# A Fourier filter and a low-rank mixer on one core: half of the inverse table copied on GpSimd, batch 1's x loaded behind the filters, U prepared earlier

## The chip, the cores and the metric

The kernel runs on one core of a Trainium2 chip. The engines of a core work side by side, each through its own instructions in order: TensorE (PE, matrix products into PSUM), VectorE (DVE), ScalarE (ACT), GpSimd (POOL) and SyncE (SP). POOL and SP also issue the DMAs. The metric is device time in microseconds (us), the median of several executions; lower is better. One further execution was recorded by the hardware profiler.

## The reference

`x` has 8 batches of 3136 x 256 values.

```python
X = np.fft.rfft(x, axis=1)                       # along the 3136
y = np.fft.irfft(X * (filt_r + 1j * filt_i), n=3136, axis=1)
h = y.transpose(0, 2, 1) @ U @ V                 # U: 3136 x 32, V: 32 x 3136
u = y + h.transpose(0, 2, 1)
out = u + np.maximum(u @ w_ch1, 0) @ w_ch2       # 256 -> 1024 -> 256
```

## The kernel before, in words

The transform of length 3136 is done as 64 x 49 by matrix products in float16. **Stage 1** (`pa` for batch 0, `pf` for the others) multiplies x by a 64-point table, `w64`. **Stage 2** (`px`) multiplies by one table per frequency s, `t2`; there are 32 values of s, taken two at a time, so a batch has 16 pairs m = 0 to 15. Then the product with the filters `ft` on VectorE (`uv`), and the inverse of stage 2 (`pi`) with the table `g12`. The inverse of stage 1 is joined with the low-rank part in `make_u`, which gives u (`ut`); `mm1` and `mm2` are the two channel products.

For the product, the real and imaginary halves stand in partitions 0 to 63 and 64 to 127. Batches 0 and 1 multiply by the real and the imaginary filter in one instruction (`both_products`), and apply the inverse with two tables: g and gs, which is g with its halves of partitions swapped. In `g12` g and gs alternate, 98 columns each for every s. Only batches 0 and 1 read gs.

**Loads.** All large loads go through POOL's queue, in the order of the program: x of batch 0 in three chunks (8, 8 and 9 columns of rows); the last rows of the filters; then four parts of eight s each (`PARTS`, lines 231 to 239), every part with its t2, four loads of filters and one load of g12. Batch 1's x comes as `load_x(1, 0)` ahead of the last part, `load_x(1, 1)` and `load_x(1, 2)` behind it, then U (`uq`, with a memset on POOL ahead), V, and the channel weights. `load_table` (178), `load_filters` (185) and `load_x` (146) issue them. Each part of the filters is copied to the other partitions by VectorE (`swap_real` line 213, `swap_imag` line 220) when the pairs reach it.

**Batch 0** (`first_f1`, then `first_mid`, 381). For every pair m the order is: VectorE's product; `back(m - 1)`, the inverse of the pair before (`pi` L395, copied to `et` by ScalarE L398); `ahead(m + 2)`, stage 2 (`px` L488); `first_a(m + 3)`, transposes (`pt` L376, copied by ScalarE L378). From pair 7 on one unit of batch 1's stage 1 is put behind each pair by `next(fill)`. `f1_units` (440) is a generator with 13 units: units 0 to 3 read chunk 0 of x, 4 to 7 chunk 1, 8 to 12 chunk 2. A unit is one product `pf` (L449) and one copy to `asb` (L453 on VectorE, L455 on ScalarE); `asb` has two buffers, one per chunk, and behind the last unit of a chunk SyncE stores it to DRAM (`c1`, L459). The products go to the PSUM tag "o", which has two banks, as do `pt` and `prep_u`'s `pu`.

**The turn** follows the last pair: 25 columns are transposed back (`pe` L432) in seven groups, copied to `e2` by VectorE and ScalarE (L433); behind the second group stands `prep_u` (303), which transforms U (L311, L321), and behind groups 1 to 4 the last four units. Then `h1_unit` (`ph` L566) forms the low-rank part of batch 0 and `make_u(0)` the first u (`pu` L618 and L624, two copies to `ut` L676).

**Then the main loop**, from `mm1` L683 on: two pairs of instructions of `mm1` and `mm2` alternate with units of later batches at slots (`sched`). Batch 1's pairs start at slot 8, in the second group of rows. Their input `a` (L469, SyncE) is read from `c1`, and each of its loads reads rows of all three chunks; SyncE issues its DMAs in order.

Of the kernel before, what the change touches and what calls it, by code (L numbers as in the profile page):

```python
# [26 lines left out]
def _consts():  # L27
    n, half = SEQ, SEQ // 2
    r = np.array([8 * (k // 4) + 4 * h + k % 4 for h in range(2) for k in range(NH - h)])
    q = np.arange(NQ)  # L30


    w = np.zeros((NQ, NS, 2))
    for s in range(NS):
        w[:, s, 0] = np.cos(2 * np.pi * s * q / NQ)
        w[:, s, 1] = -np.sin(2 * np.pi * s * q / NQ)
    w[:, 0, 1] = (-1.0) ** q
    w = w.reshape(NQ, 64)
    turn = np.arange(64).reshape(4, 16).T.ravel()
    w64 = np.zeros((128, 128))  # L40
    w64[:64, :64] = w
    w64[64:, 64:] = w
    s2 = np.zeros((128, 128))
    s2[:64, :64] = w.T / ESC
    s2[64:, 64:] = w.T / ESC


    t2 = np.zeros((NS, 98, 128))
    g = np.zeros((NS, 128, 98))
    for s in range(NS):  # L50
        for j in range(49):
            if j < 25:
                f = s + 64 * j
                e, sg = np.exp(-2j * np.pi * f * r / n), 1.0
            elif s:
                f = 64 * (j - 24) - s
                e, sg = np.exp(-2j * np.pi * (n - f) * r / n), -1.0
            else:
                f = 32 + 64 * (j - 25)
                e, sg = np.exp(-2j * np.pi * f * r / n), 1.0  # L60
            ei = np.conj(e)
            if s:
                t2[s, :49, j], t2[s, 49:, j] = e.real, -e.imag
                t2[s, :49, 64 + j], t2[s, 49:, 64 + j] = sg * e.imag, sg * e.real
                g[s, j] = np.concatenate([ei.real, ei.imag]) * 2
                g[s, 64 + j] = np.concatenate([-ei.imag, ei.real]) * 2 * sg
            else:
                o = 0 if j < 25 else 49
                t2[s, o:o + 49, j] = e.real
                t2[s, o:o + 49, 64 + j] = e.imag  # L70
                g[s, j, o:o + 49] = ei.real * (2 if f else 1)
                g[s, 64 + j, o:o + 49] = -ei.imag * 2

    t2[0, :, 64] = 0
    t2[0, 49:, 64] = (-1.0) ** r
    g[0, 64] = 0
    g[0, 64, 49:] = (-1.0) ** r
    g *= ESC / n
    gs = np.concatenate([g[:, 64:], g[:, :64]], 1)
    f16 = np.float16  # L80
    return (w64.astype(f16), s2.astype(f16), np.eye(128).astype(f16),
            np.tile(np.eye(32), (4, 4)).astype(f16),
            np.pad(np.hstack([w[:, turn], w[:, turn].T / ESC]), ((0, 64), (0, 0))).astype(f16),
            np.ascontiguousarray(t2.reshape(4, 8, 98, 128).transpose(0, 2, 1, 3)).astype(f16),
            np.ascontiguousarray(np.stack([g, gs], 1).reshape(4, 8, 2, 128, 98)
                                 .transpose(0, 3, 1, 2, 4)).astype(f16))


@with_exitstack
def kernel(  # L90
# [10 lines left out]
):  # L101
    nc = tc.nc
    nb = x.shape[0]
    w64_np, s2_np, idn_np, fold_np, wp_np, t2_np, g_np = _consts()
    w64_d = nc.inline_tensor(w64_np, name="w64d")
    s2_d = nc.inline_tensor(s2_np, name="s2d")
    idn_d = nc.inline_tensor(idn_np, name="idnd")
# [1 line left out]
    wp_d = nc.inline_tensor(wp_np, name="wpd")  # L109
    t2_d = nc.inline_tensor(t2_np, name="t2d")  # L110
    g_d = nc.inline_tensor(g_np, name="gd")
    RD = NR * DM
    c1 = [nc.dram_tensor(f"c1_{b}", (64, RD), F16, kind="Internal") for b in range(nb)]
    c2 = [nc.dram_tensor(f"c2_{b}", (64, RD), F16, kind="Internal") for b in range(nb)]
# [62 lines left out]

    def load_table(k, a, b):

        dst, src, w = ((t2, t2_d, 128), (g12, g_d, 196))[k]  # L180
        n, p = (b - a) * w, dst.shape[0]
        nc.gpsimd.dma_start(dst[:, a * w:b * w],
                            bass.AP(tensor=src, offset=a // 8 * p * n, ap=[[n, p], [1, n]]))

    def load_filters(a, b):

# [42 lines left out]
    s2 = cst.tile([128, 128], F16)  # L229
    nc.sync.dma_start(s2, s2_d.ap())  # L230
    for k, part in enumerate(PARTS):
        if k == 3:
            load_x(1, 0)
        if k:
            load_table(0, *part)
        load_filters(*part)
        if k == 0:
            load_table(0, *part)
        load_table(1, *part)
    load_x(1, 1)  # L240
    load_x(1, 2)
    uq = sb.tile([128, NR * RANK], F16, tag="esb", bufs=2, name="uq")
    nc.gpsimd.memset(uq[64:128, :], 0.0)
    nc.gpsimd.dma_start(uq[0:64, :], moe_U.rearrange("(q r) p -> q (r p)", q=NQ))
    vqs = []
    for k in range(2):
        v = sb.tile([128, SEQ // 2], F16, tag="xt", bufs=5, name="vq")
# [55 lines left out]
    def prep_u():  # L303
        usb = sb.tile([128, NH * RANK], F16, tag="uv", bufs=3, name="usb")
        st[0]["usb"] = usb
        nc.vector.memset(usb[64:128, (NH - 1) * RANK:NH * RANK], 0.0)
        for n0, nn in ((0, 16), (16, 9)):
            pu = bank("o", "pu")
            for h in range(2):
                k = nn // 4  # L310
                nc.tensor.matmul(  # L311
                    pu[64 * h:64 * h + 64, 0:4 * k * RANK], w64[0:64, 0:64],
                    bass.AP(tensor=uq.tensor, offset=uq.offset + (2 * n0 + 4 * h) * RANK,
                            ap=[uq[0:64, :].ap[0], [8 * RANK, k], [1, 4 * RANK]]),
                    start=True, stop=True, skip_group_check=True)
            if nn % 4:
                nc.tensor.matmul(pu[0:64, (nn - 1) * RANK:nn * RANK], w64[0:64, 0:64],
                                 uq[0:64, (NR - 1) * RANK:NR * RANK],
                                 start=True, stop=True, skip_group_check=True)
            m = (min(nn, NH - 1 - n0)) * RANK  # L320
            nc.scalar.copy(usb[:, n0 * RANK:n0 * RANK + m], pu[:, 0:m])  # L321
            if m < nn * RANK:
                nc.vector.tensor_copy(usb[0:64, n0 * RANK + m:(n0 + nn) * RANK],
                                      pu[0:64, m:nn * RANK])
# [56 lines left out]
    def first_mid(fill):  # L381
# [5 lines left out]
        def back(m, uv):  # L387
            pi = bank("fx"[m % 2], "pi")
            for sl in range(2):
                for dh in range(2):  # L390
                    for fi in range(2):
                        g = (4 * m + 2 * sl + fi) * 98
                        o = fi * 512 + sl * DM + dh * 128
                        a = (dh * 2 + sl) * 98
                        nc.tensor.matmul(pi[:, a:a + 98], uv[:, o:o + 128], g12[:, g:g + 98],  # L395
                                         start=(fi == 0), stop=(fi == 1), skip_group_check=True)
            for h in range(2):
                nc.scalar.copy(  # L398
                    etv[:, h, :, 0:NH - h, 4 * m:4 * m + 4],
                    pi[:, 0:392].rearrange("p (e k r) -> p e r k", e=2, r=NR)  # L400
                    [:, :, h * NH:h * NH + NH - h])
# [6 lines left out]
        for m in range(NS // 2):  # L408
            for k, part in enumerate(PARTS):
                if k and 2 * m == part[0]:  # L410
                    swap_real(*part)
                    swap_imag(*part)
            uv = both_products(m, pxs.pop(0))
            if pend is not None:
                back(*pend)
            pend = (m, uv)
            if m + 2 < NS // 2:
                pxs.append(ahead(m + 2))
            if m + 3 < NS // 2:
                first_a(m + 3)  # L420
            if m >= 7:
                next(fill)
        back(*pend)
        e2 = new_e2(0, 0)
        for k4, n0 in enumerate(range(0, NH, 4)):
# [3 lines left out]
            for rr in range(w):  # L429
# [2 lines left out]
                    nc.tensor.transpose(pt[0:k, o:o + 128], et[:, a:a + k], idn[:, :])  # L432
            (nc.scalar.copy if k4 in (1, 4, 6) else nc.vector.tensor_copy)(  # L433
                split(e2[0:k, n0 * DM:(n0 + w) * DM]), natural(pt[0:k, 0:w * DM]))
            if k4 == 1:
                prep_u()
            if k4 in (1, 2, 3, 4):
                next(fill)

    def f1_units(b, both):  # L440
        ne = 0
        for c in range(len(CH)):
            xt = st[b]["x"].pop(c)
            asb = sb.tile([128, 9 * DM], F16, tag="asb", bufs=2, name="asb")
            for n0 in range(0, CH[c], 2):
# [3 lines left out]
                nc.tensor.matmul(pf[:, 0:w], w64[:, :], xt[:, n0 * DM:n0 * DM + w],  # L449
                                 start=True, stop=True)  # L450
                dst = asb[0:k, n0 * DM:n0 * DM + w]
                if both and ne % 2 and (b > 1 or ne >= 9):
                    nc.vector.tensor_copy(dst, pf[0:k, 0:w])  # L453
                else:
                    nc.scalar.copy(dst, pf[0:k, 0:w])  # L455
# [59 lines left out]
    def stream():  # L515
        pend = []

        def i1(b, m, y, esb):
            pi = bank("f", "pi")
            nf = 2 if b == 1 else 1  # L520
            for sl in range(2):
                for fi in range(nf):
                    g, o = (4 * m + 2 * sl + fi) * 98, fi * 512 + sl * DM
                    nc.tensor.matmul(pi[0:98, sl * DM:(sl + 1) * DM], g12[:, g:g + 98],  # L524
                                     y[:, o:o + DM], start=(fi == 0), stop=(fi == nf - 1),
                                     skip_group_check=True)
# [121 lines left out]
    def make_u(gx):  # L648
# [11 lines left out]
        for dh in range(2):  # L660
# [12 lines left out]
                nc.scalar.copy(dst.rearrange("p (k h r t) -> p k h r t", k=2, h=2, r=4),  # L673
                               pm.rearrange("p (r h k t) -> p k h r t", r=4, h=2, k=2))
            else:
                nc.scalar.copy(dst, pm)  # L676

    def mm1(gx, t):
        w = groups[gx][2] * 128
# [105 lines left out]
    h1gen = h1_unit(0)  # L785
    next(h1gen)
    make_u(0)

    steps = [7.6 + 1.3 * k for k in range(NP)] + [28 + 2.45 * k for k in range(NP)]
    for b in range(3, nb):  # L790
# [86 lines left out]
```

## Time and profile before

| what | value |
|---|---|
| runs | 539.4, 538.82, 539.82 us; median 539.4 |
| the profiled execution | 541.74 us, its span 540.0 us |
| mean granted TensorE clock | 0.982 |
| TensorE busy | 501.7 us, 93% of the span, 4022 products |
| VectorE, ScalarE, GpSimd busy | 400.1, 377.3, 288.5 us |
| DMA | 94.58 MB, mean 175 GB/s |
| chain that ended last | TensorE 76%, VectorE 9%, DMA 6%, ScalarE 4% |

The span runs from the first to the last instruction of the profiled execution; 541.74 us is its whole time. Times in the views count from the start of the span. In the slices of the page each digit is a fortieth of the span (13.5 us), in tenths; PEclk is the clock that TensorE was granted, 9 being 0.9 or more. In a timeline the number in brackets is how long the engine stood idle ahead of the instruction, and what ended that.

### The profile page before, as it was taken

How to read it: one execution, taken by the hardware profiler on the slowest of the kernel's cores; microseconds unless marked ns; L12 is line 12 of the kernel's file. 1: busy time of each engine (PE TensorE's matmuls, PEld its weight loads, DVE VectorE, ACT ScalarE, POOL GpSimd, SP SyncE). 2: the span in 40 equal slices, each digit the busy share in tenths (PEclk: the TensorE clock that was granted, in tenths of full speed). 3: DMA queues.
4: the chain of work that ended last, by engine and by line, in shares of the span. 5: the costliest groups of instructions: out<-in, count | busy, mean ns of one | idle time of the engine just before them, and what ended most of it. 6: DMA issues, size and time to landing. Idle time of an engine off the chain costs nothing.

```text
span 540.0 us, 11365 instructions
## 1 busy us (share of the span) xinstructions
PE 501.7 (93%) x4022; PEld 305.3 (57%) x4022; DVE 400.1 (74%) x576; ACT 377.3 (70%) x768; POOL 288.5 (53%) x406
## 2 busy tenths in 40 slices
PE   3856899999999999999999999999999999999995
PEld 3745557767666776555555555555555555454444
DVE  6876367676887767887888878887899887336664
ACT  2746676667676768878878878887777777775541
POOL 7657634344466455666677657774656565313000
PEclk9968799999999999999999999999999999999999
DMA  8999898966988649997989788996786684554324
GB/s 132 179 179 191 163 207 226 199 205 171 239 195 226 183 97 252 213 221 179 202 205 233 192 170 214 208 226 150 187 197 159 133 189 116 133 109 80 73 67 104
DMA packets 118426, 94.58 MB, mean 175 GB/s; under 512 B 52961, under 2 KB 100770, under 8 KB 118370
## 3 DMA queue, kind: packets, MB, share of 16 engines
q0 software_dynamic: 21936, 42.52, 39.6%
q1 hardware_dynamic: 96434, 51.35, 37.8%
q8 instruction: 31, 0.51, 0.4%
q14 instruction: 25, 0.20, 0.1%
HBM read 56.85 MB, written 48.17 MB: 194 GB/s over the span
## 4 chain that ended last, share of the span: by engine, by line
PE 76%; DVE 9%; DMA 6%; ACT 4%; issue 3%; POOL 1%; DVEq 0%; ACTq 0%; SPq 0%; POOLq 0%
PE phh L683 26%; PE po L739 20%; PE po L709 8%; PE px L488 5%; PE pi L524 4%; DVE uv L509 4%; PE pu L609 3%; PE pf L449 3%; DMA xt<-in_x_dram 3%; PE ph L566 2%; ACT h L691 2%; DVE uv L507 2%; DMA g<-gd 2%; DMA c<-asb 1%; PE po L713 1%
## 5 line engine op out<-in xcount | busy, mean ns | idle before, releaser
L691 ACT ACTIVATE h<-phh 128x512 f16<-128x512 f32 (+1 forms) x382 | 201.6, 578 | 73.7 <-PE phh L683 69.2
L683 PE MATMUL phh<-ut,w 128*128 128x512 f16 x768 | 197.6, 379 | 1.0 <-ACT ut L676 0.5
L512 POOL TENSOR_TENSOR y<-uv 128x512 f16<-128x512 f16 x96 | 113.2, 1180 | 108.8 <-DVE uv L509 71.4
L739 PE MATMUL po<-h,w 128*128 128x512 f16 x560 | 143.8, 379 | 0.0
L509 DVE TENSOR_TENSOR uv<-px,ft 64x512 f16<-64x512 f32 x192 | 132.1, 688 | 2.6
L683 PEld LDWEIGHTS <-w 128*128 128x128 f16 x832 | 78.4, 98 | 77.8 <-issue 3.1
L752 POOL DMA_DIRECT2D out_dram<-och x120 | 69.7, 588 | 46.5 <-DVE och L744 43.3
L528 ACT CAST esb<-pi 98x512 f16<-98x512 f32 x112 | 65.9, 588 | 37.8 <-PE pi L524 34.3
L507 DVE TENSOR_TENSOR uv<-px,ft 128x512 f16<-128x512 f32 x96 | 64.8, 675 | 36.2 <-PE px L488 34.0
L739 PEld LDWEIGHTS <-w 128*128 128x128 f16 x560 | 51.6, 98 | 53.2 <-issue 1.1
L743 DVE TENSOR_TENSOR tt<-po,ut 128x512 f32<-128x512 f32 x70 | 48.4, 692 | 41.3 <-PE po L739 30.1
L709 PE MATMUL po<-w,h 128*128 128x256 f16 x448 | 58.1, 273 | 0.0
L488 PE MATMUL px<-a,t 98*128 98x256 f16 x256 | 50.3, 278 | 6.7 <-DVE uv L509 4.7
L455 ACT CAST asb<-pf 128x512 f16<-128x512 f32 (+1 forms) x83 | 48.0, 579 | 10.6 <-PE pf L449 7.6
L744 DVE STREAM_TRANSPOSE och<-tt 128x512 f32<-128x512 f32 x70 | 49.8, 711 | 2.4
L709 PEld LDWEIGHTS <-h 128*128 128x128 f16 x448 | 42.5, 98 | 10.3 <-issue 1.1
L496 DVE TENSOR_TENSOR uv<-px,ft 128x1024 f16<-128x1024 f32 x32 | 38.2, 1220 | 12.3 <-PE px L488 11.9
L488 PEld LDWEIGHTS <-t 98*128 98x128 f16 x256 | 22.1, 100 | 34.8 <-DVE uv L509 17.0
L449 PE MATMUL pf<-xt,w 128*128 128x512 f16 (+1 forms) x91 | 35.0, 386 | 5.4 <-DMA xt<-in_x_dram 4.6
L673 ACT CAST ut<-pu 128x512 f16<-128x512 f32 x70 | 38.1, 608 | 0.7 <-PE pu L609 0.7
L524 PE MATMUL pi<-y,g 128*98 128x256 f16 x192 | 36.7, 272 | 0.5 <-POOL y L512 0.5
L153 POOL DMA_DIRECT2D xt<-in_x_dram x50 | 30.3, 612 | 5.1 <-DMA xt<-in_x_dram 2.4
(92 smaller groups left out, 448.1 us busy)
## 6 DMA issues: line engine op xcount, KB each, us to landing
xt<-in_x_dram POOLq DMA_DIRECT2D x46, 256.0 KB, 6.8
a<-c SPq DMA_DIRECT2D x28, 384.0 KB
c<-esb SPq DMA_DIRECT2D x28, 384.0 KB
e<-c SPq DMA_DIRECT2D x56, 192.0 KB
out_dram<-och SPq DMA_DIRECT2D x160, 64.0 KB
c<-asb POOLq DMA_DIRECT2D x30, 256.0 KB, 4.2
out_dram<-och POOLq DMA_DIRECT2D x120, 64.0 KB, 3.3
out_dram<-och POOLq DMA_DIRECT2D x24, 256.0 KB, 5.3
```

The source lines that it names most:

```text
L449: nc.tensor.matmul(pf[:, 0:w], w64[:, :], xt[:, n0 * DM:n0 * DM + w], start=True, stop=True)
L488: nc.tensor.matmul(px[:, sl * DM:(sl + 1) * DM], t2[:, s * 128:(s + 1) * 128], a2[:, (2 * ml + sl) * DM:(2 * ml + sl + 1) * DM], start=Tru ...
L507: nc.vector.tensor_mul(uv[:, 0:512], px[:, :], ft[:, a:a + 512])
L509: nc.vector.tensor_mul(uv[p:p + 64, 512:1024], px[q:q + 64, :], ft[q:q + 64, b:b + 512])
L512: nc.gpsimd.tensor_add(y, uv[:, 0:512], uv[:, 512:1024])
L524: nc.tensor.matmul(pi[0:98, sl * DM:(sl + 1) * DM], g12[:, g:g + 98], y[:, o:o + DM], start=(fi == 0), stop=(fi == nf - 1), skip_group_che ...
L528: nc.scalar.copy(split(esb[:, ml * 512:(ml + 1) * 512]), natural(pi[0:98, :]))
L683: nc.tensor.matmul(pm[:, 0:w], w1[:, dh * 1024 + t * 128:dh * 1024 + (t + 1) * 128], ut[:, dh * w:(dh + 1) * w], start=(dh == 0), stop=(dh ...
L691: nc.scalar.activation(h[:, 0:w], pm[:, 0:w], RELU)
L709: nc.tensor.matmul(po[:, o:o + DM], hs[gx, t][:, rr * 128:(rr + 1) * 128], w2[:, t * DM:(t + 1) * DM], start=(t == 0), stop=False, skip_gr ...
L739: nc.tensor.matmul(po[:, :], w2[:, t * DM + dh * 128:t * DM + (dh + 1) * 128], hs[gx, t][:, :], start=(t == 0), stop=(t == 7))
L752: (nc.gpsimd if k and b < nb - 1 else nc.sync).dma_start(dst, och[32 * i:32 * i + 32, k * 512:(k + 1) * 512] .rearrange("p (r e) -> p r e" ...
```

## The change

- `g12` holds all of g first and all of gs behind it. Only part 0 of gs is loaded; for parts 1 to 3 POOL copies the two halves of g to the swapped partitions (`swap_table`: two copies of 64 partitions x 784 elements a part), each part's copies being one part later in POOL's order than its load.
- `load_x(1, 0)` moves behind the last part; U's load comes right behind it, and its memset goes to VectorE. The last swap stands ahead of `load_x(1, 2)`.
- Units of batch 1's stage 1 start at pair 9. Unit 7 and `prep_u` come ahead of the last `back`, units 8 and 9 behind groups 2 and 4 of the turn, and units 10 to 12 behind `make_u(0)`.
- VectorE copies units 8 to 11 (before 9 and 11), the second part of `usb` and the second half of the first `ut`, which ScalarE copied before.

```diff
     def load_table(k, a, b):
-        dst, src, w = ((t2, t2_d, 128), (g12, g_d, 196))[k]
+        dst, src, w = ((t2, t2_d, 128), (g12, g_d, 98))[k]
 ...
+    def swap_table(a, b):
+        o = NS * 98
+        for p, q in ((0, 64), (64, 0)):
+            nc.gpsimd.tensor_copy(g12[p:p + 64, o + a * 98:o + b * 98],
+                                  g12[q:q + 64, a * 98:b * 98])
 ...
     for k, part in enumerate(PARTS):
-        if k == 3:
-            load_x(1, 0)
         if k:
             load_table(0, *part)
         load_filters(*part)
         if k == 0:
             load_table(0, *part)
         load_table(1, *part)
+        if k == 0:
+            nc.gpsimd.dma_start(g12[:, NS * 98:(NS + 8) * 98], gs_d.ap())
+        if k > 1:
+            swap_table(*PARTS[k - 1])
+    load_x(1, 0)
+    uq = sb.tile([128, NR * RANK], F16, tag="esb", bufs=2, name="uq")
+    nc.vector.memset(uq[64:128, :], 0.0)
+    nc.gpsimd.dma_start(uq[0:64, :], moe_U.rearrange("(q r) p -> q (r p)", q=NQ))
     load_x(1, 1)
+    swap_table(*PARTS[3])
     load_x(1, 2)
-    uq = sb.tile([128, NR * RANK], F16, tag="esb", bufs=2, name="uq")
-    nc.gpsimd.memset(uq[64:128, :], 0.0)
-    nc.gpsimd.dma_start(uq[0:64, :], moe_U.rearrange("(q r) p -> q (r p)", q=NQ))
 ...                                                    # prep_u
-            nc.scalar.copy(usb[:, n0 * RANK:n0 * RANK + m], pu[:, 0:m])
+            (nc.vector.tensor_copy if n0 else nc.scalar.copy)(usb[:, n0 * RANK:n0 * RANK + m], pu[:, 0:m])
 ...                                                    # first_mid: back; the same in i1
-                        g = (4 * m + 2 * sl + fi) * 98
+                        g = (fi * NS + 2 * m + sl) * 98
 ...                                                    # first_mid: the pairs and the turn
-            if m >= 7:
+            if m >= 9:
                 next(fill)
+        next(fill)
+        prep_u()
         back(*pend)
 ...
-            if k4 == 1:
-                prep_u()
-            if k4 in (1, 2, 3, 4):
+            if k4 in (2, 4):
                 next(fill)
 ...                                                    # f1_units
-                if both and ne % 2 and (b > 1 or ne >= 9):
+                if both and (ne % 2 if b > 1 else 8 <= ne < 12):
 ...                                                    # make_u
-                nc.scalar.copy(dst, pm)
+                (nc.vector.tensor_copy if gx == 0 and dh else nc.scalar.copy)(dst, pm)
 ...                                                    # after the first u
     make_u(0)
+    for k in range(3):
+        next(fill)
```

More of the change, by code (lines that the diff above doesn't have):

```diff
@@ L84, in _consts @@
             np.ascontiguousarray(t2.reshape(4, 8, 98, 128).transpose(0, 2, 1, 3)).astype(f16),
-            np.ascontiguousarray(np.stack([g, gs], 1).reshape(4, 8, 2, 128, 98)
-                                 .transpose(0, 3, 1, 2, 4)).astype(f16))
+            np.ascontiguousarray(g.reshape(4, 8, 128, 98).transpose(0, 2, 1, 3)).astype(f16),
+            np.ascontiguousarray(gs[0:8].transpose(1, 0, 2)).astype(f16))
 @with_exitstack
@@ L103 @@
     nb = x.shape[0]
-    w64_np, s2_np, idn_np, fold_np, wp_np, t2_np, g_np = _consts()
+    w64_np, s2_np, idn_np, fold_np, wp_np, t2_np, g_np, gs_np = _consts()
     w64_d = nc.inline_tensor(w64_np, name="w64d")
@@ L111 @@
     g_d = nc.inline_tensor(g_np, name="gd")
+    gs_d = nc.inline_tensor(gs_np, name="gsd")
     RD = NR * DM
@@ L522, in i1 @@
                 for fi in range(nf):
-                    g, o = (4 * m + 2 * sl + fi) * 98, fi * 512 + sl * DM
+                    g, o = (fi * NS + 2 * m + sl) * 98, fi * 512 + sl * DM
                     nc.tensor.matmul(pi[0:98, sl * DM:(sl + 1) * DM], g12[:, g:g + 98],
```

## The prediction

> **What bounds the kernel now.** I read the page's slices first. Before slice 6 (13.5 us each) TensorE has gaps and loses its clock; behind it TensorE is almost full, and the windows view gives it 445.45 us busy of the 460 us from 80 to 540. So the change, which touches the first 75 us alone, is worth what it shifts the start of that full stretch.
>
> ```profile
> PE   3856899999999999999999999999999999999995
> PEclk9968799999999999999999999999999999999999
> ```
>
> Then TensorE's timeline of that stretch (start, length, engine, operation, in brackets the idle time ahead and what ended it):
>
> ```profile
> 36.93 0.61 PE L449 MATMUL pf<-xt,w 128*128 128x512 f16 x1 [4.11 <-DMA xt<-in_x_dram]
> ...
> 40.77 0.63 PE L449 MATMUL pf<-xt,w 128*128 128x512 f16 x1
> ...
> 52.46 1.76 PE L432 MATMUL pe<-idn,et 128*128 128x128 f16 x16 [3.58 <-ACT et L398]
> ...
> 55.81 0.59 PE L449 MATMUL pf<-xt,w 128*128 128x512 f16 x1 [0.78 <-ACT usb L321]
> ...
> 60.42 1.19 PE L566 MATMUL ph<-e,usb 128*32 128x256 f16 x25
> ...
> 72.20 0.38 PE L488 MATMUL px<-a,t 98*128 98x256 f16 x2
> ```
>
> Three gaps: the first unit of batch 1 stands in pair 7 and waits 4.11 us for batch 1's x; the turn waits 3.58 us; `prep_u` holds it for another 0.78. ScalarE's timeline names the cause of the second, unit 8, which waits for the store of chunk 0 to free its `asb` buffer, with the last `et` copy queued behind it:
>
> ```profile
> 51.37 0.59 ACT L455 CAST asb<-pf 128x512 f16<-128x512 f32 x1 [2.13 <-DMA c<-asb]
> ```
>
> Then the DMA issues, one window for each issue, which give issue and landing; the second half of `load_x(1, 0)` is issued at 28.33 and lands 8.6 later, at 36.93:
>
> ```profile
> xt<-in_x_dram POOLq DMA_DIRECT2D x1, 256.0 KB, 8.6
> ```
>
> From such rows POOL's loads land one behind the other, in the order of issue: the first 8 filters by 18.2, t part 0 18.9, g 0 21.5, t 1 22.7, filters 1 25.5, g 1 28.0, t 2 28.9, filters 2 32.7, g 2 34.2, x(1,0) 36.9, t 3 38.0, filters 3 40.6, g 3 42.4, x(1,1) 44.5, x(1,2) 47.1. POOL issues a load as soon as the one eight places ahead has landed (27th 21.85 after the 19th at 21.5, 33rd 28.33 after the 25th at 28.0), so the transfers are the bound and not the issuing.
>
> **The change part by part: table and x.** A part of g shrinks from 392 to 196 KB. t has 196 KB, and its steps above are 0.7, 1.2, 0.9 and 1.1 us; I take 1.1. The g steps are 2.6, 2.5, 1.5 and 1.8, so each part saves 0.4 to 1.5, together with g 2 some 2.2. Part 0 gains nothing (g and gs, two loads for one). x(1,0) now comes behind t 3 (1.1), filters 3 (2.6) and a halved g 3 (1.1): 36.9 + 4.8 - 2.3 = 39.4. It is needed in pair 9 instead of 7. Against pair 9's unit in the old run (40.77) that is 1.4 us sooner. TensorE still stands idle there, from about 35.5 (pair 8's product is ready at 34.5, one DVE step of 1.2 behind the filters' swap that ends at 33.3; its inverse and the transforms behind it take 1) to 39.4.
>
> **The copies.** No POOL copy here changes partitions, so the price is bounded by three rows:
>
> ```profile
> L272 POOL COPY low<-vq 32x256 f16<-32x256 f16 x12 | 8.2, 725 | 2.8 <-DMA vq<-in_moe_V_dram 2.8
> ...
> L549 POOL COPY low<-wp 64x448 f16<-64x448 f16 x7 | 3.9, 570 | 0.1
> ...
> L781 POOL COPY w<-w2n 128x1024 f16<-128x1024 f16 x2 | 2.0, 1033 | 2.5 <-DMA w2n<-in_moe_w_ch_dram 2.5
> ```
>
> The last two give 0.8 ns an element and 0.21 us fixed: 0.84 for 784 elements. At L272's 2.8 ns it would be 2.2; at no less than 570 for 448 it can't go under 0.57. I take 0.84, the contiguous rows being the nearest: 1.7 a swap. Swap 1 waits on POOL for g 1, now 26.7, and ends at 28.5; queued behind it are t 3 and all of filters 3. Pair 4's product ends at 28.3 already, so its inverse starts about 0.2 late, which DVE, two pairs ahead, hides. Swap 2 waits for g 2 (about 32) and ends at 34; pair 8 needs it at 34.4. Behind it are the x loads: issued at 34.1 and 34.7, they find three or four microseconds of filters still in the queue, so 39.4 stands. Swap 3 ends near 39, and pair 12 needs it after 41; queued behind it are x(1,2), V and the weights. V is issued at 42.95 now; the swaps fill POOL's waits for landings, the transfers ahead are 2.3 shorter and the memset is gone, so it will be issued no later, while its readers come at most 4 sooner; V's copies end at 59.3 now and only their first rows are needed for the first u. The memset of `uq` goes from POOL (1.43) to DVE, where it falls into the idle 3.11 us ahead of 14.07; uncovered it would cost 0.7 (a DVE memset of 32x1024 words is 0.91).
>
> The copies also meet DVE's own copies. One row shows such a meeting: the swap of filters at 41.84 took 1.03 instead of 0.69 beside POOL's memset (40.88 to 42.31). DVE has over a microsecond to spare at the swaps of parts 2 and 3, as TensorE waits for x. POOL can be held as well: 0.3 at swap 1 (DVE's copies end at 27.0, g 1 lands at 26.7) and 0.8 at swap 2 (DVE's end at 33.3, POOL's begin at 32.5), 1.1 for four copies, which the queue still covers. The Trainium skill (SBUF — State Buffer, section Who interferes with whom) says that such a DVE copy and a GpSimd instruction lock each other out of a shared port for a whole instruction, which speaks against this change. By that rule the row would have been 1.16, so the trace nearly agrees.
>
> **From pair 9 to the turn.** Pairs 10 and 11 go at the slow clock's step, as the old ones did (36.93, 38.83, 40.77): 1.9 each. Pair 12 is bound by ScalarE's three copies, 1.6; 13 lacks `first_a`, 1.1; 14 and 15 take 0.95 (asb and the et copies, 47.21 to 48.11). That is 8.4 to unit 6, at 47.8. Then ScalarE has et, two asb, a usb and the last et to do, with `prep_u` on TensorE between, as its two banks come free: 3.3. The first transposes start at 51.1, 1.4 before the old 52.46. The wait for chunk 0's store is gone, since unit 8 now stands in the turn.
>
> **The turn** took 60.5 - 52.46 = 8.0. `prep_u` leaves it (54.28 to 55.81, 1.5) and two of four units (0.43 and 0.11). At half clock throughout it would be 50 transposes (0.85 for 8) and two units: 6.2. At full clock DVE's six copies of 0.69 and their dispatch bind: 4.9. I take 5.2. Gain 2.8; `ph` starts 4.2 sooner.
>
> **Beside the first u.** Three units now stand between `make_u(0)` and the first `phh`. They have two banks: unit 12 waits until DVE has copied u's second half (0.69) and unit 10 (0.69). On the old clock times: u's second half ready 63.5, DVE done with unit 10 at 64.95, unit 12 on TensorE to 65.1, then `phh`, then unit 12's copy on ScalarE, and the first h at 65.8 instead of 64.76. Loss 1.0; the copy of u halved between two engines (0.5) is in it.
>
> **Who waits next.** Batch 1's `a` loads need the whole of c1, so they come behind the store of the last chunk. SyncE's timeline:
>
> ```profile
> 61.04 1.08 SPq L459 DMA_DIRECT2D c<-asb  x2
> 65.35 5.17 SPq L469 DMA_DIRECT2D a<-c  x6
> ```
>
> The store went out when unit 12 was copied (61.02), 3.7 before the first h; the loads 4.3 later; their queue shows the first tile's 512-byte packets until about 69.5, so it is there by 69.9, 2.3 ahead of the `px` at 72.20. Now unit 12 is copied at the first h. The slack of 2.3 turns into a wait of 1.4 (0 to 2.5).
>
> **Sum.** 1.4 + 2.8 - 1.0 - 1.4 = 1.8 sooner. The profiled execution took 541.74 (span 540.0); the runs' median is 539.4, 2.3 less. 541.74 - 1.8 = 539.9, less 2.3: 537.6. A change of 0.2% (1.1 us) is about what can be told from none.
>
> **Rivals.** *The clock stays full.* TensorE's granted clock fell to 0.55 in 52 to 59, after the gap of 3.58, and the gaps left in the turn are under 1 us; but it also fell (0.59 from 28 to 32) after a gap of 1.3. If only long gaps count, the turn is 4.9, and with pair 9's wait a little shorter pairs 10 and 11 go at 1.6: 0.3 + 0.6 more, 536.7. The Trainium skill (TensorE: Matmul & The Clock Gate, Part 1) has this rule: half clock after a whole idle window of about 3.4 us. By that rule the old turn agrees, and the drop at 28 doesn't. Chance 0.2.
>
> *The late units eat it all.* If the last store shares the queue with x(2,1), which is issued at about the same time, `a` lands another 1 to 2 us later; that leaves -0.2 to 0.8, in the middle 539.1. For it: both queues' packets lie close together from 61 to 69 now. Chance 0.14.
>
> *The copies hold up POOL.* At 2.2 us a copy (L272's rate) swap 1 ends at 31.2, swap 2 at 39.3, the filter queue runs dry, and x(1,0), issued at 39.3 and 39.9, lands 4.0 later (as lightly queued x loads do at 63): 43.9, 4.5 later than in the forecast, with TensorE idle all the while: 537.6 + 4.5 = 542.1, slower. It decides from 0.84 + 1.8 / 4 = 1.3 us a copy, four copies being ahead of x. For it: the change of partitions, and DVE's copies, which alone bring a copy to 0.84 + 1.1 / 4 = 1.12; against it: the rows of 570 and 1033. Chance 0.24, half copies included.
>
> **How the numbers follow.** Forecast 0.42, with its own range 536.9 to 538.4 (transfer steps and the turn's bounds); clock 0.2, eaten 0.14, copies 0.24. Faster 0.62, same 0.14, slower 0.24. The range reaches from 535.0 (clock, and no wait for `a`) to 541.0 (copies of about 1.7 us).
>
> **What would show it.** Right: POOL copies near 0.84; unit 0 in pair 9 waiting 3 to 4 us for x until about 39.4; no ScalarE wait for c in the turn; transposes from about 51; `phh` about 3 sooner; `px` waiting 1 to 2 for `a`. Wrong: copies over 1.3, x after 41, or no wait at `px`.

## The result, and the profile after

The new kernel's median is 541.21 us (11 runs) against 538.81 for the old one in the same rounds: ratio 1.0052, 95% interval 1.0029 to 1.0074. It is slower by some 2.4 us; 537.6 was forecast. Two later rounds gave 1.0050 (1.0027 to 1.0072) and 1.0038 (1.0008 to 1.0068). The old kernel measured against itself gave 1.0036 (1.0008 to 1.0063) and 1.0004 (0.9972 to 1.0036), so a single ratio may stray by more than its interval says; three of the same sign stand. The ratios use undisturbed executions alone, so they are not the quotients of the medians beside them.

The profiled execution of the new kernel took 540.77 us, 0.4 under its median, its span 538.8. The page's slices again:

```profile
PE   4758879999999999999999999999999999999995
PEclk9989899999999999999999999999999999999999
```

Laid beside the slices of before, they do not show a slower kernel: the clock is lost for less time. TensorE's timeline (start, length, operation, idle time ahead and what ended it):

```profile
39.02 0.59 PE L461 MATMUL pf<-xt,w 128*128 128x512 f16 x1 [4.45 <-DMA xt<-in_x_dram]
...
50.00 1.51 PE L446 MATMUL pe<-idn,et 128*128 128x128 f16 x24 [0.64 <-ACT et L410]
...
55.59 0.38 PE L578 MATMUL ph<-e,usb 128*32 128x256 f16 x5 [0.79 <-DVE e L447]
...
59.14 0.27 PE L461 MATMUL pf<-xt,w 128*128 128x256 f16 x1 [0.84 <-DVE asb L465]
...
71.29 0.39 PE L500 MATMUL px<-a,t 98*128 98x256 f16 x2 [2.54 <-DMA a<-c]
```

Unit 0 waits for x until 39.02, the transposes begin at 50.0 (forecast: 39.4 and 51.1), unit 12 waits for its bank, `px` waits 2.54 for `a`: much of the forecast's picture. Against the recorded old execution `px` is 0.9 us sooner (71.29 against 72.20). The runs say the opposite, so the recorded old execution is what has to be looked at.

GpSimd's copies, from the groups of its operations (count, busy us, mean ns, idle ahead), and SyncE's timeline:

```profile
L190 POOL COPY g<-g 64x784 f16<-64x784 f16 x6 | 5.7, 947 | 0.3
```

```profile
59.88 1.08 SPq L471 DMA_DIRECT2D c<-asb  x2
67.42 2.46 SPq L481 DMA_DIRECT2D a<-c  x6
```

Unit 8's wait for chunk 0's store has moved from ScalarE to VectorE and is smaller (in the two other recordings of the new kernel, below, it is 0.27 and nothing):

```profile
53.05 0.69 DVE L465 CAST asb<-pf 128x512 f16<-128x512 f32 x1 [0.80 <-DMA c<-asb]
```

### The profile page after: what moved, and what is told of

Same layout as the page of the kernel before. It is cut to its first block, busy times and chain, and to the rows that moved or that the text cites. A ratio compares the mean times of both kernels' runs of the same rounds, so it can differ in the third digit from the quotient of the medians.

```text
span 538.8 us, 11373 instructions
## 1 busy us (share of the span) xinstructions
PE 499.2 (93%) x4022; PEld 302.0 (56%) x4022; DVE 403.1 (75%) x581; ACT 375.4 (70%) x764; POOL 293.7 (55%) x412
## 4 chain that ended last, share of the span: by engine, by line
PE 74%; DVE 10%; DMA 6%; ACT 4%; issue 3%; POOL 3%; SPq 0%; DVEq 0%; ACTq 0%; POOLq 0%
PE phh L695 26%; PE po L751 19%; PE po L721 8%; PE px L500 5%; PE pi L536 4%; DVE uv L521 4%; PE pu L621 3%; PE pf L461 3%; DMA xt<-in_x_dram 2%; DVE uv L519 2%; PE ph L578 2%; ACT h L703 2%; DMA c<-asb 1%; DMA ft<-in_filt_r_dram 1%; PE po L725 1%
## 5 line engine op out<-in xcount | busy, mean ns | idle before, releaser
L703 ACT ACTIVATE h<-phh 128x512 f16<-128x512 f32 (+1 forms) x382 | 201.8, 578 | 74.7 <-PE phh L695 69.9
L467 ACT CAST asb<-pf 128x512 f16<-128x512 f32 (+1 forms) x81 | 46.9, 582 | 10.8 <-PE pf L461 10.7
L721 PEld LDWEIGHTS <-h 128*128 128x128 f16 x448 | 42.5, 98 | 10.3 <-issue 1.1
L461 PE MATMUL pf<-xt,w 128*128 128x512 f16 (+1 forms) x91 | 33.8, 375 | 5.8 <-DMA xt<-in_x_dram 4.4
L621 PEld LDWEIGHTS <-e 96*128 96x128 f16 x686 | 26.5, 98 | 10.7 <-DVE e L589 1.7
```

Of the source, the lines that this page charges most:

```text
L703: nc.scalar.activation(h[:, 0:w], pm[:, 0:w], RELU)
L721: nc.tensor.matmul(po[:, o:o + DM], hs[gx, t][:, rr * 128:(rr + 1) * 128], w2[:, t * DM:(t + 1) * DM], start=(t == 0), stop=False, skip_gr ...
```

## The experiments

Each run here took 12 executions (the first comparison 11), one of them recorded. Kernels of a round ran in turn on one chip, with the old one between them. In the table "x" is when unit 0 of batch 1 starts on TensorE, "store" when the last store of c1 is issued, "px" batch 1's first `px`, all from the one recorded execution, whose time is in the second column; "rest" is its span less px. That execution can lie some us above or below the median: those of the first old one, `a_table`, `s_slot` and `m_early` took 2.2 to 2.9 us more than the median, those of `u_late` and `n_loaded` 1.9 to 2.4 less, and that of `ctl_before` 3.6 less, so their times of x, store and px are not typical ones.

| kernel | recorded | x | store | px (its wait for a) | rest | median, ratio (interval) |
|---|---|---|---|---|---|---|
| old, first recorded | 541.74 | 36.93 | 61.04 | 72.20 (0) | 467.8 | 538.81 |
| old, `c_before` | 538.13 | 33.49 | 54.09 | 67.66 (2.25) | 468.7 | 539.37, 1.0036 (1.0008 to 1.0063) |
| old, `ctl_before` | 536.18 | 33.15 | 54.56 | 66.56 (0.68) | 467.8 | 539.82, 1.0004 (0.9972 to 1.0036) |
| new, first recorded | 540.77 | 39.02 | 59.88 | 71.29 (2.54) | 467.5 | 541.21, 1.0052 (1.0029 to 1.0074) |
| new, `c_after` | 541.23 | 38.85 | 60.56 | 70.88 (2.73) | 468.2 | 541.10, 1.0050 (1.0027 to 1.0072) |
| new, `ctl_after` | 541.50 | 39.10 | 60.10 | 70.73 (3.03) | 468.8 | 541.31, 1.0038 (1.0008 to 1.0068) |
| `a_table` | 541.02 | 33.83 | 57.53 | 71.28 (2.44) | 468.0 | 538.31, 0.9990 (0.9958 to 1.0022) |
| `b_turn` | 537.32 | 38.72 | 56.91 | 68.11 (0.66) | 467.5 | 537.40, 0.9975 (0.9958 to 0.9993) |
| `u_late` | 538.93 | 32.64 | 58.01 | 68.49 (2.84) | 468.6 | 541.31, 1.0015 (0.9991 to 1.0039) |
| `n_loaded` | 539.72 | 37.72 | 58.94 | 69.17 (1.38) | 468.4 | 541.63, 1.0026 (1.0006 to 1.0045) |
| `s_slot` | 541.55 | 38.99 | 60.17 | 73.80 (0) | 465.6 | 539.32, 0.9994 (0.9971 to 1.0017) |
| `m_early` | 542.76 | 34.58 | 53.49 | 70.88 (0) | 469.9 | 540.06, 1.0001 (0.9976 to 1.0025) |
| `l_turn` | 537.96 | 39.01 | 56.60 | 67.66 (0.52) | 468.4 | 538.84, 0.9997 (0.9968 to 1.0026) |
| `p_early` | 537.16 | 32.24 | 54.69 | 66.62 (1.40) | 468.5 | 537.50, 0.9980 (0.9950 to 1.0009) |

`c_before`, `c_after`, `a_table` and `b_turn` shared a round (the old kernel's median beside them 538.08), as did `u_late` to `m_early` (540.12), and `ctl_before`, `ctl_after`, `l_turn` and `p_early` (539.48). Medians compare within these three groups.

**The old kernel again.** No edit.

> The old kernel again, unchanged. Theory one (the recorded execution of the old kernel was a late one: 541.74 us against a median of 538.81, while the new one's, 540.77, was no later than its median of 541.21): most executions of the old kernel reach batch 1's first px two to three microseconds sooner than 72.2, so at 69 to 70.5, because x(1,0) lands sooner or the clock is lost for less time; span about 537. Theory two (the start is as recorded, and the loss of the new kernel lies behind px, in the main loop): px again at 72.2 +- 0.5, and the stretch from px to the end is shorter than the 467.8 recorded for the old kernel. Ratio 1.000 either way.

TensorE's timeline of this execution:

```profile
33.49 0.39 PE L449 MATMUL pf<-xt,w 128*128 128x512 f16 x1 [1.42 <-DMA xt<-in_x_dram]
...
47.95 1.07 PE L432 MATMUL pe<-idn,et 128*128 128x128 f16 x16 [1.37 <-ACT et L398]
...
67.66 0.38 PE L488 MATMUL px<-a,t 98*128 98x256 f16 x2 [2.25 <-DMA a<-c]
```

Theory one holds: x is there 3.4 us sooner than in the first recording, the gap ahead of the turn is 1.37 instead of 3.58, and `px` comes at 67.66, sooner than the 69 to 70.5 expected, and already waits for `a`. This execution took 1.2 us less than the median of its run, so it is itself a somewhat early one. The ratio of 1.0036 was not expected.

**The new kernel again.** No edit.

> The new kernel again, unchanged. Both theories: ratio 1.003 to 1.007. Theory one: px at 71 to 72, having waited 2 to 3 us for a, and 467.5 +- 0.7 us from px to the end, as recorded (538.8 - 71.3). Theory two: from px to the end 469 or more.

px at 70.88 (0.1 under the expected band), 468.2 behind it (at the band's upper end), against 468.7 and 467.8 in the old kernel. Nothing is lost in the main loop that these recordings show; the difference stands in when px starts, on average 71.0 in three recordings of the new kernel and 67.1 in the two further ones of the old. Already the first `phh` starts at 59.25 to 59.92 in the new kernel's three, against 56.91 and 57.38 in the old one's two.

**The table alone** in the old kernel (`swap_table` and the columns of `g12` as in the change).

```diff
-        dst, src, w = ((t2, t2_d, 128), (g12, g_d, 196))[k]
+        dst, src, w = ((t2, t2_d, 128), (g12, g_d, 98))[k]
...
+        if k == 0:
+            nc.gpsimd.dma_start(g12[:, NS * 98:(NS + 8) * 98], gs_d.ap())
+        if k > 1:
+            swap_table(*PARTS[k - 1])
     load_x(1, 1)
+    swap_table(*PARTS[3])
```

> The table alone: halved g, gs copied by GpSimd; x(1,0) stays ahead of the last part, the units in pairs 7 to 15, prep_u and the last units in the turn. If the saved transfers count, x(1,0) lands about 2.2 sooner than in the old kernel, the wait in pair 7 shrinks by that, and the ratio is 0.996 to 0.998. If GpSimd's copies hold up what is queued behind them (measured 0.85 to 1.0 a copy, so 1.7 to 2.1 a swap), x is no sooner: 1.000. If the copies are what makes the new kernel slower: above 1.003.

x lands at 33.6, no sooner than in the old kernel (33.1 and 33.3 in the two further recordings), though its second half is issued only at 28.84 (25.6 and 26.1 there), behind the first swap. Unit 0 starts at 33.83 without a wait, and the ratio is 0.9990: the second of the three outcomes by the time of x. The ratio alone does not exclude the first, as its interval reaches from 0.9958 to 1.0022.

**The three late units back in the turn.**

```diff
-            if k4 in (2, 4):
+            if k4 in (2, 3, 4, 5, 6):
                 next(fill)
...
     make_u(0)
-    for k in range(3):
-        next(fill)
```

> The new kernel with units 10 to 12 back in the turn (units 8 to 12 behind groups 2 to 6), none behind make_u(0). Theory of the late a (the new kernel loses at px, where it waited 2.5 us, and 1 us at the first h): the turn grows by 1 to 1.5 (three units more on VectorE and ScalarE), the wait at px shrinks from 2.5 to under 0.7, the first h comes 1 us sooner behind make_u(0); the time falls by 1.5 to 2.5 against the new kernel, ratio 0.998 to 1.003. If the loss lies elsewhere (the main loop, the copies), the ratio stays at 1.004 to 1.006.

The last store leaves 3.6 us sooner than in `c_after`, `px` waits 0.66 instead of 2.73 and comes 2.8 sooner; the median falls by 3.7 in the same round, and the ratio of 0.9975 is just below the expected band. SyncE's and TensorE's lines:

```profile
56.91 1.09 SPq L471 DMA_DIRECT2D c<-asb  x2
68.11 0.38 PE L500 MATMUL px<-a,t 98*128 98x256 f16 x2 [0.66 <-DMA a<-c]
```

The late units are the part of the change that costs.

**The late units alone** in the old kernel.

```diff
-            if k4 in (1, 2, 3, 4):
+            if k4 == 1:
                 next(fill)
...
     make_u(0)
+    for k in range(3):
+        next(fill)
```

> The old kernel with one thing alone: units 10 to 12 behind make_u(0) instead of in the turn. Theory of the late a (batch 1's first px starts when the chain last unit, store, loads of a is through; the later last unit moves px, and everything behind px only shifts): the last store goes out 4 to 6 us later than in the old kernel seen from the first phh, px waits 4 to 6 us for a (old kernel: 0 and 2.3 in two recorded executions), ratio 1.004 to 1.010. Rival (the new kernel's copies and x order cost, the late units don't): the turn is 1 us shorter and the ratio is 0.998 to 1.002.

The wait is 2.84, less than expected, and the ratio 1.0015 leaves no clear verdict. The last store leaves 3.5 to 3.9 later than in the old kernel's two further recordings, but `px` follows it by 10.5 instead of 12.0 to 13.6. So a cost of the late units by themselves is not shown, nor excluded (the interval ends at 1.0039); within the new kernel, where x is late as well, they cost what `b_turn` shows. The late x alone was not run.

**All of gs loaded, nothing copied.** (`gs_d` then holds all of gs.)

```diff
-        if k == 0:
-            nc.gpsimd.dma_start(g12[:, NS * 98:(NS + 8) * 98], gs_d.ap())
-        if k > 1:
-            swap_table(*PARTS[k - 1])
+        a, n = part[0], 8 * 98
+        nc.gpsimd.dma_start(g12[:, (NS + a) * 98:(NS + a + 8) * 98],
+                            bass.AP(tensor=gs_d, offset=k * 128 * n, ap=[[n, 128], [1, n]]))
...
-    swap_table(*PARTS[3])
```

> The new kernel with all of gs loaded and none copied: everything else of the change as it is. If the saved transfers count as forecast, x(1,0) lands 2 to 2.5 us later than the new kernel's 38.9, at 41 to 41.5, and the ratio is 1.008 to 1.011. If GpSimd's copies let the queue of transfers run thin (the DMA share over 30 to 40 us is 0.90 in the new kernel and 1.15 in the old one), x lands within 1 us of 38.9 and the ratio is that of the new kernel, 1.004 to 1.007.

Unit 0 has x at 37.72, 1.3 sooner than in the first new recording with 588 KB more ahead of it, so the saved transfers saved nothing. The windows view of 20 to 40 us (busy time and instructions of each engine; the last three columns are granted clock, DMA share and GB/s), the old kernel (`ctl_before`), the new one (`ctl_after`) and this one in turn:

```profile
20.00:40.00 20.00, 13.43 (x173) 11.04 (x171) 19.45 (x19) 13.74 (x38) 14.41 (x24) 0.97 1.14 193
```

```profile
20.00:40.00 20.00, 12.86 (x160) 10.81 (x158) 19.57 (x20) 11.57 (x32) 18.41 (x28) 0.91 0.89 152
```

```profile
20.00:40.00 20.00, 14.55 (x168) 12.21 (x168) 19.39 (x21) 12.87 (x34) 16.38 (x28) 0.87 1.08 201
```

With copies the DMA engines carry 152 GB/s, without them 193 and 201; the seven recordings with copies lie between 151 and 161, the others between 192 and 209, the first old recording at 169. Part of the difference is the saving itself: 588 KB over 20 us are 29 GB/s. For the rest GpSimd's timeline of the new kernel shows a place: no load is issued while the copies run.

```profile
25.32 0.62 POOL L183 DMA_DIRECT2D g<-gd  x1
25.99 1.71 POOL L190 COPY g<-g 64x784 f16<-64x784 f16 x2
27.64 0.59 POOL L183 DMA_DIRECT2D t<-t2d  x1
...
30.57 0.82 POOL L183 DMA_DIRECT2D g<-gd  x1
31.43 2.02 POOL L190 COPY g<-g 64x784 f16<-64x784 f16 x2
33.39 1.21 POOL L154 DMA_DIRECT2D xt<-in_x_dram  x2
```

x, issued at 33.4 and 34.0, finds an almost empty queue (the last load ahead of it lands at 34.5), and its second half lands 4.9 later (7.2 to 8.6 in the three old recordings, behind a full one). Without the copies x is issued 2.9 and 2.4 us sooner and takes longer, 6.0 for the second half:

```profile
30.53 0.67 POOL L154 DMA_DIRECT2D xt<-in_x_dram  x1
31.57 0.83 POOL L154 DMA_DIRECT2D xt<-in_x_dram  x1 [0.37 <-DMA t<-t2d]
```

In time, 1.0026 is under the expected band and under the new kernel's ratios, but those come from other rounds; what the copies cost in the end is open.

**Batch 1's pairs two slots later.**

```diff
-    steps = [7.6 + 1.3 * k for k in range(NP)] + [28 + 2.45 * k for k in range(NP)]
+    steps = [10 + 1.14 * k for k in range(NP)] + [28 + 2.45 * k for k in range(NP)]
```

> The new kernel with batch 1's pairs put from slot 10 (step 1.14) instead of 7.6 (1.3): the first px stands two slots later in TensorE's order, behind products of the channel layers. If what is lost is TensorE standing idle in front of px, the wait of 2.5 us shrinks to under 1 and the time falls by 1 to 2 us against the new kernel: ratio 1.001 to 1.004. If the loss is in when the stream of batch 1 starts and not in TensorE's idling (its pairs then meet later slots), the ratio stays at 1.004 to 1.007.

px stands at 73.80 and waits for nothing; the rest is 465.6, so TensorE did other work meanwhile. The ratio, 0.9994, is under the expected band, which speaks for TensorE's idle time ahead of px as what the new kernel loses. The new kernel did not run in this round, and the same shift was not tried in the old kernel, where px can wait for `a` too.

**x early, with the rest of the change.** `b_turn` with

```diff
+        if k == 3:
+            load_x(1, 0)
...
-    load_x(1, 0)
+    load_x(1, 1)
     uq = sb...
-    load_x(1, 1)
     swap_table(*PARTS[3])
...
-            if m >= 9:
+            if 7 <= m < 15:
                 next(fill)
-        next(fill)
         prep_u()
```

> A combination: the new table, U and the split copies; x(1,0) ahead of the last part and x(1,1) ahead of U, units 0 to 7 in pairs 7 to 14, units 8 to 12 in the turn, none behind make_u(0). Theory of the late a: the last unit and so the last store go out 2 to 3 us sooner than in the kernel with the units back in the turn (56.9), a and px as much sooner (px at 65 to 66.5 against 68.1): ratio 0.992 to 0.996. If the chain is not bound by the units but by the queue of transfers (the store and a behind the channel weights), px stays at 67.5 to 68.5: 0.997 to 0.999.

The last store goes out at 53.49, sooner than in any other kernel, and `px` is no sooner for it (70.88). In this execution other transfers take the place: the first `phh` waits for the channel weights, a unit of batch 2 for its x.

```profile
57.80 1.05 PE L695 MATMUL phh<-ut,w 128*128 128x512 f16 x4 [2.57 <-DMA w<-in_moe_w_ch_dram]
64.73 0.38 PE L461 MATMUL pf<-xt,w 128*128 128x512 f16 x1 [2.04 <-DMA xt<-in_x_dram]
```

It was the longest of its twelve, 2.7 us over the median, so whether these waits stand in the others is not shown. The ratio of 1.0001 shows no gain either way.

**Controls, and the change without its two suspects.** `l_turn` joins the edits of `n_loaded` and `b_turn`; `p_early` is `l_turn` with the x order of `m_early`.

> The old kernel unchanged, beside the three others on one chip, as the measure of how far the ratio strays by itself (it was 1.0036 once): 0.997 to 1.003. The recorded execution: x(1,0) at 33 to 37, px at 67.5 to 72.5, 467.5 to 468.7 behind it.

> The new kernel unchanged on the same chip: 1.003 to 1.007, px at 70.5 to 71.5 after a wait of 2 to 3 us for a.

> The new kernel with both suspects out: all of gs loaded (no copies on GpSimd) and units 8 to 12 in the turn (none behind make_u(0)). Theory that both cost (the copies thin the queue of transfers, the late units hold up the last store): x at 37.7 as in the kernel with loaded gs, the last store at 55.5 to 56.5, px at 66.5 to 67.5, ratio 0.994 to 0.997. If the copies cost nothing in the end, it equals the kernel with the units back in the turn, 0.9975.

> As the last, but x(1,0) ahead of the last part as in the old kernel, units 0 to 7 in pairs 7 to 14. If the units' chain is the bound: the last store at 52.5 to 53.5 and px 1 to 2 us sooner than in the last kernel, ratio 0.991 to 0.995. If the transfers as a whole bind (filters, weights, x of batch 2, stores and a all pass the same queues before px), another transfer takes the place, the channel weights at the first phh or batch 2's x, px stays at 67 or later, and the ratio is no lower than the last kernel's.

In the old control x is at the early end of the band and px 0.9 sooner than it:

```profile
33.15 0.39 PE L449 MATMUL pf<-xt,w 128*128 128x512 f16 x1 [2.44 <-DMA xt<-in_x_dram]
...
66.56 0.39 PE L488 MATMUL px<-a,t 98*128 98x256 f16 x2 [0.68 <-DMA a<-c]
```

It was the shortest of its twelve executions. `l_turn` has px at 67.66 and 2.5 us less than the new kernel in the same round, a ratio of 0.9997, over the band expected: what is left of the change shows no gain against the old kernel. x came at 39.01, not at 37.7, so the gain of 1.3 by loading gs was not repeated. `p_early` has px at 66.62; its 0.9980 is the best of this group, yet neither clear of 1 nor of `l_turn`. It is over the expected band of 0.991 to 0.995, and no variant beats the old kernel beyond what the old one strays against itself.

## Why the prediction was wrong

**The step that failed is the base of the sum**, in two places of the prediction.

First, "541.74 - 1.8 = 539.9, less 2.3: 537.6". The excess of 2.3 us of the recorded execution over the median was carried through as if it lay evenly over the span or beyond the change. It lay in the very stretch that the change touches: the recorded old start reached px at 72.2, two others at 67.66 and 66.56, with the rest equal to a microsecond. In the recorded one the loads moved 159 and 179 GB/s in the slices 20 to 30 and 30 to 40, against 192 and 195 in `c_before`. So the waits to be removed (4.11 for x, 3.58 ahead of the turn) were in large part that execution's own: they are 1.42 and 2.44 for x, and 1.37 both times ahead of the turn, in the two others. Those two lie 1.2 and 3.6 below the medians of their runs, so a typical start lies between them and the first: with the 468.1 behind px and the 1.8 outside the span, the old medians of the four rounds (538.08 to 540.12) put px at an estimated 68 to 70, the new ones at 71.

The new kernel itself was forecast nearly right: px at 72.2 - 1.8 = 70.4, measured 71.29, 70.88 and 70.73. So of the 3.6 us between 537.6 and the median of 541.21 the subtraction of 2.3 is the larger part, the later px 0.3 to 0.9; the rest lies behind px and outside the span. Some of the closeness of px is luck, as the points below show: the first `phh` came sooner and the wait for `a` was longer than forecast.

Second, "so it is there by 69.9, 2.3 ahead of the `px` at 72.20". In both other recordings of the old kernel px waits for `a`, 2.25 and 0.68: there is no slack of 2.3. From the issue of the store to `a` the prediction had 8.9 (61.04 to 69.9); measured to px, behind a wait for `a`, it is 10.3 to 11.4 in the new kernel and 12.0 and 13.6 in those two of the old. There the chain x, last unit, store, `a`, px is the bound already, and a sooner turn or a sooner first `phh` is worth nothing unless the store and `a` come sooner too.

By that chain the loss can be read off. In the old kernel's two further recordings the store follows x by 20.6 and 21.4, px follows the store by 13.6 and 12.0. In the new one x comes some 5.7 us later (39.0 against 33.3), the store follows it by 20.9, 21.7 and 21.0, and px follows that by 11.4, 10.3 and 10.6. What two pairs fewer between x and the last unit would save is used up by putting that unit behind `make_u(0)`; only the shorter way from store to px gives something back. That makes 71.0 - 67.1 = 3.9 later by the recordings; the medians differ by only 1.8 to 3.0, as the two old recordings were early ones.

**Point by point.**

- Table: "together with g 2 some 2.2" saved was wrong. The prediction's own steps give 1.4 for g 1 and 0.4 for g 2, and of these nothing arrives: x did land near the forecast's time (39.4 forecast, 38.9 to 39.1 measured), but it does so with all of gs loaded too (37.7 and 39.0). The time came right for another reason. The prediction's sentence that the x loads "find three or four microseconds of filters still in the queue" was the error: in the first new recording all that stood ahead had landed by 34.5, 1.1 behind the issue of x. So x comes when it does because GpSimd, busy with its copies, issues it later, which uses up what fewer bytes ahead of it save.
- Copies: 0.84 was forecast, 0.95 measured, 1.71 to 2.08 a swap (2.15 at most in the other two recordings). The rival that they hold up POOL was right in kind, but not in its price (1.3 a copy), nor in x coming after 41.
- DVE beside POOL: its filter copies took 1.10 and 1.32 at 36.6 and 37.7 instead of 0.69, under the wait for x, as forecast. The Trainium skill (SBUF — State Buffer, section Who interferes with whom) says that the later of the two is blocked; the trace agrees in kind, as GpSimd's pair beside them takes 2.08 instead of the 1.71 of the first swap.

```profile
36.62 1.10 DVE L221 COPY ft<-ft 64x2048 f16<-64x2048 f16 x1
37.65 1.32 DVE L228 TENSOR_SCALAR ft<-ft 64x2048 f16<-64x2048 f16 x1
```

- From pair 9 to the turn: 8.4 + 3.3 forecast, 50.0 - 39.0 = 11.0 measured.
- The turn: 5.2 forecast; `ph` begins at 53.45, 3.45 behind the first transposes, but waits for `e` until 55.59; in the first new recording 0.80 of this is unit 8's wait for chunk 0's store on VectorE. "The wait for chunk 0's store is gone" did not hold there: that store takes until 53 to land. In `c_after` the wait is gone.
- Beside the first u: bank wait as forecast (0.84 at unit 12).
- "`phh` about 3 sooner": it is 3.9 to 4.6 sooner than in the first old recording (63.86), and 1.9 to 3.0 later than in the two others.
- px's wait for `a`: 1.4 (0 to 2.5) forecast, 2.5 to 3.0 measured.
- The clock: in the old kernel's other recordings it is full or nearly so from 20 to 40 (1.00 and 0.97, against 0.80 in the first), so that rival's gain, like the forecast's, was measured against an untypical start.
- *The late units eat it all* was the right rival by its outcome: `a` came later than forecast, and with the base corrected the change ends well past zero. Its mechanism, the last store sharing the queue with batch 2's x, is not shown: the way from store to px is no longer in the new kernel than elsewhere.

## What to carry to other kernels

When a recorded execution is slower than the median, find where its excess lies before summing against it: here it lay in the waits that the change was to remove. Ask of every slack whether the next execution has it as well, and follow the chain of transfers (load, unit, store, reload) as a path of its own beside TensorE's. An engine that issues loads and also copies trades bytes against the depth of the queue; here fewer bytes were no gain, as the loads behind the copies were issued later.

## What was not expected of the hardware

Replacing three loads of 196 KB by copies on the engine that issues the loads lowered the traffic from about 200 to 152 GB/s over 20 us, some 29 of that being the bytes saved, and x came no sooner. The same program's loads moved at 159 GB/s in one execution and 189 to 192 in two others over the same slice (20 to 30 us), and its px stood 4.5 to 5.6 us later; why that execution's transfers were slower no run here shows.
